# New due times for the steps behind the first weight loads in a fused attention and feed-forward kernel

## The chip, the cores and the metric

One Trainium2 chip, one of its cores. The metric is device microseconds (us) of one execution, the median of a few runs; lower is better. The profile is of one execution on that core.

## What is computed

A gated linear attention (RWKV style) over 4 batches, 8 heads, 768 positions and 48 values a head, whose output goes straight into a two-layer feed-forward net with 3072 tokens, width 384 and 2048 hidden values:

```python
for t in range(S):
    cur = np.einsum('bhd,bhe->bhde', u[None] * kt, vt)
    y[:, :, t] = np.einsum('bhd,bhde->bhe', rt, state + cur)
    state = wt[:, :, :, None] * state + np.einsum('bhd,bhe->bhde', kt, vt)
x = y.transpose(0, 2, 1, 3).reshape(B * S, H * D)
h = x @ w_in
g = np.maximum(0.01 * h, h)
return g @ w_out
```

Inputs and output are float32 in DRAM; the products run in bf16 and are summed in float32.

## The kernel before, in words

The 768 positions of each batch are cut into 6 chunks of 128, so there are 24 chunks, numbered in the order in which they are worked on. Chunks 0 to 3 are done two at a time (`pair`), chunks 4 to 23 one at a time (`single`). The work on a chunk of `single` is a chain over five engines:

1. SP issues four loads of 192 KB (w, k, r, v; L755) into one of 10 `in` tiles.
2. ACT takes the logarithm of w (`lw`, L765); PE sums it along the chunk (L771, L774, the step `cum`); DVE forms `ci` (L783); ACT takes the exponentials (L792, L797, L801); DVE multiplies them with r and k (L459).
3. The products are turned around, either on PE (L470, `tpose`) and copied out by DVE or ACT (L475, L477), or by a transposing DMA that SP issues (L818; the set `RK_DMA` says for which chunks).
4. PE forms the scores (L912), DVE masks them (L842, two instructions a chunk), PE forms the chunk's output (L878, L883, the step `intra`). Beside it PE forms the sum for the state (L852, `sums`), DVE adds it to the state (L867) and POOL scales the state for the next chunk of the batch (L829).
5. POOL works out the bonus term of u: `ru` (L489, L493), then DVE a reduction `dg` (L497), then POOL `vs` (L501); POOL also casts v (L509). DVE adds `vs` to the output (L532) and the sum y is turned into a column of `xT`, by PE (L518, the step `typose`, and a copy L523 or L525) or by a transposing DMA (L897; the set `Y_DMA`).

The feed-forward net works on blocks of one or two chunks: `up` (L1074) needs the block's columns of `xT`, ACT applies the leaky relu (L1089), `down` (L1104) sums over 16 products in four steps, DVE or ACT copies the result into one of 5 `o` tiles (L1115, L1117), and SP stores it (L1121). The last three blocks of two chunks each save one of eight products (`seven`: L1006 on PE, sums L989 on DVE, the final additions L1027 and copies L1020 and L1022, stores L1057). For them DVE forms differences of the weights beforehand (L958, four instructions).

No loop sets the order of all this. Every piece is a step (1089 of them) with the engines that may do it, an assumed duration, a due time and its dependencies. `Plan.order` plays the steps through once at build time: whenever an engine is free it takes the ready step with the lowest due time, and this gives the order in which the instructions are written into each engine's queue. Each engine then works its own queue strictly in that order, and an instruction that waits holds up all behind it. The table `RANK` is added to the due times by step number, and `FORCE` fixes the engine of some steps; a step without an entry keeps the due time that the code gave it:

```python
for i, x in RANK.items():
    plan.steps[i][2] = round(plan.steps[i][2] + x, 3)
for i, e in FORCE.items():
    plan.steps[i][0] = {e: plan.steps[i][0][e]}
order = plan.order(pools)
```

Two more things matter below. A transfer of SP goes into one queue of the DMA engines; in the middle of the kernel it lands about 4 us after its issue. And the PSUM tiles `ps` are 8 banks of 512 floats: in `seven`, one bank holds two results side by side (`px` and `py` in the first, `pv` and `pw` in the second).

Of the kernel before, what the change touches and what calls it, by code (L numbers as in the profile page):

```python
# [23 lines left out]
class Plan:  # L24
# [202 lines left out]
FORCE = {23: "DVE", 26: "DVE", 29: "ACT", 30: "DVE", 46: "ACT", 58: "ACT", 61: "ACT", 79: "ACT", 85: "DVE",  # L227
    112: "DVE", 114: "ACT", 117: "DVE", 119: "ACT", 121: "ACT", 123: "DVE", 125: "POOL", 127: "ACT", 128:
    "POOL", 134: "POOL", 137: "DVE", 139: "POOL", 142: "ACT", 143: "POOL", 492: "DVE", 500: "ACT", 604: "DVE",
    612: "ACT", 904: "DVE", 910: "DVE", 932: "ACT", 952: "ACT", 966: "ACT", 1002: "ACT", 1030: "ACT", 1075:  # L230
    "ACT", 1080: "ACT"}


@with_exitstack
# [946 lines left out]
```

## Time and profile before

| | us |
|---|---|
| median of 3 runs (180.39 to 180.79) | 180.65 |
| the profiled execution | 181.35 |
| its span, first to last instruction | 179.64 |
| PE busy in the span | 172.6 |
| DVE busy | 132.2 |
| ACT busy | 115.7 |
| POOL busy | 104.0 |

The profiled execution is 0.70 us above the median, and 1.71 us of it lie outside the span. "Busy" of PE counts the modelled end of each matmul, which overlaps the start of the next; what PE loses is therefore read from the starts of the matmuls: where one group begins later than the group before it takes elsewhere, PE has waited. SP's transfers are issued one behind the other from the start up to about 154 us; the share of the DMA engines in part 2 of the page is the packets' time, not their peak rate.

### The profile page before, as it was taken

What the parts mean: (1) busy time and instruction counts of PE and PEld (TensorE: products, weight loads), DVE (VectorE), ACT (ScalarE), POOL (GpSimd) and SP (SyncE); (2) the same over time, 40 slices, a digit from 0 to 9 for tenths busy, and PEclk for the clock granted to TensorE, in tenths of its full rate; (3) what the DMA queues carried; (4) which work ended last, traced back from release to release, by engine and by line L of the source; (5) the groups of instructions that cost most, each with busy time, mean ns of one, the idle gap of its engine ahead of it and who ended that gap; (6) DMA issues with size and microseconds to landing.
All of it is one profiled execution on the core that took longest, in us unless ns stands there. A gap on an engine that the chain in (4) does not pass through costs nothing.

```text
span 179.6 us, 5374 instructions
## 1 busy us (share of the span) xinstructions
PE 172.6 (96%) x2109; PEld 135.2 (75%) x2109; DVE 132.2 (74%) x265; ACT 115.7 (64%) x257; POOL 104.0 (58%) x138
## 2 busy tenths in 40 slices
PE   7998999999999999999999999999999999999991
PEld 2475878867878687787688777677778798899991
DVE  7589974189788898559687659499787599777472
ACT  2568968865957786895379775177675487735620
POOL 5989631675896486878468855414995459200000
PEclk9999999999999999999999999999999999999999
DMA  5999999999999989999899999999599996613004
GB/s 139 261 283 314 370 380 362 176 203 208 215 195 202 192 192 150 183 199 182 193 214 177 218 164 214 212 192 144 117 201 145 198 234 170 153 24 115 0 22 153
DMA packets 116715, 34.43 MB, mean 192 GB/s; under 512 B 109137, under 2 KB 115922, under 8 KB 116690
## 3 DMA queue, kind: packets, MB, share of 16 engines
q1 hardware_dynamic: 116688, 34.09, 90.8%
q8 instruction: 16, 0.26, 0.6%
q14 instruction: 9, 0.07, 0.1%
q10 hardware_dynamic: 2, 0.00, 0.0%
HBM read 25.17 MB, written 4.72 MB: 166 GB/s over the span
## 4 chain that ended last, share of the span: by engine, by line
PE 64%; DVE 8%; DMA 8%; ACT 6%; issue 5%; SPq 4%; POOL 3%; DVEq 0%; ACTq 0%; POOLq 0%
PE ps L1074 26%; PE ps L1104 17%; PE ps L1006 6%; DMA in<-in_w_dram 6%; SPq L755 3%; PE ps L1146 3%; PE ps L912 2%; DMA xT<-y 2%; DVE m L842 2%; POOL ru L489 1%; DVE o L1027 1%; ACT g L1089 1%; PE ps L883 1%; ACT rkT L477 1%; DVE m L690 1%
## 5 line engine op out<-in xcount | busy, mean ns | idle before, releaser
L1074 PE MATMUL ps<-xT,w_in_b 128*128 128x256 bf16 (+1 forms) x720 | 73.1, 251 | 0.4 <-ACT xT L525 0.2
L1089 ACT ACTIVATE g<-ps 128x512 bf16<-128x512 f32 x96 | 56.4, 595 | 20.6 <-PE ps L1074 15.3
L1074 PEld LDWEIGHTS <-w_in_b 128*128 128x128 bf16 x720 | 57.7, 98 | 9.3 <-issue 0.7
L1104 PE MATMUL ps<-w_out_b,g 128*128 128x384 bf16 x288 | 56.0, 326 | 0.1
L1104 PEld LDWEIGHTS <-g 128*128 128x128 bf16 x288 | 25.7, 97 | 12.4 <-ACT g L1089 0.2
L489 POOL TENSOR_TENSOR ru<-in,ub 128x384 f32<-128x384 f32 x24 | 24.5, 1027 | 10.9 <-DMA in<-in_k_dram 10.1
L459 DVE TENSOR_TENSOR rk<-in,ps 128x384 bf16<-128x384 f32 x46 | 24.3, 548 | 7.8 <-ACT ps L797 4.2
L842 DVE TENSOR_TENSOR m<-ps,maskb 128x512 bf16<-128x512 f32 x40 | 25.4, 683 | 6.1 <-PE ps L912 5.0
L493 POOL TENSOR_TENSOR ru<-ru,in 128x384 f32<-128x384 f32 x24 | 24.6, 1030 | 2.9 <-DMA in<-in_r_dram 2.2
L829 POOL TENSOR_TENSOR sb<-s,a 128x384 bf16<-128x384 f32 x18 | 15.7, 873 | 9.5 <-ACT a L792 9.4
L501 POOL TENSOR_TENSOR vs<-in,dg 128x384 f32<-128x384 f32 x20 | 16.6, 828 | 7.1 <-DVE dg L497 4.7
L509 POOL CAST vb<-in 128x384 bf16<-128x384 f32 x24 | 12.0, 503 | 11.3 <-DMA in<-in_v_dram 7.5
L783 DVE TENSOR_TENSOR ci<-ps,lw 128x384 f32<-128x384 f32 x20 | 11.1, 554 | 4.3 <-PE ps L771 1.9
L497 DVE TENSOR_REDUCE dg<-ru 128x8 f32<-128x384 f32 x24 | 12.9, 545 | 1.0 <-POOL ru L493 0.8
L765 ACT ACTIVATE lw<-in 128x384 bf16<-128x384 f32 x20 | 10.4, 520 | 3.6 <-DMA in<-in_w_dram 3.6
L797 ACT ACTIVATE ps<-ps 128x384 f32<-128x384 f32 x20 | 9.5, 475 | 4.2 <-DVE ci L783 3.8
L532 DVE TENSOR_TENSOR y<-ps,vs 128x384 bf16<-128x384 f32 x20 | 11.1, 553 | 1.5 <-PE ps L883 0.6
L867 DVE TENSOR_TENSOR s<-ps,sb 128x384 f32<-128x384 f32 x14 | 7.7, 552 | 4.0 <-PE ps L852 2.8
L801 ACT ACTIVATE ps<-ci 128x384 f32<-128x384 f32 x20 | 9.8, 488 | 0.6 <-DVE ci L783 0.6
L1146 PE MATMUL ps<-zeros 128*128 128x128 bf16 (+1 forms) x40 | 8.7, 339 | 1.3 <-DVE zeros L332 1.3
L525 ACT COPY xT<-ps 128x384 bf16<-128x384 bf16 x11 | 5.2, 481 | 6.8 <-PE ps L518 6.7
L792 ACT ACTIVATE a<-ps 64x4 f32<-64x4 f32 x36 | 6.0, 168 | 5.3 <-DVE ci L783 3.5
(105 smaller groups left out, 228.7 us busy)
## 6 DMA issues: line engine op xcount, KB each, us to landing
out_dram<-o SPq DMA_DIRECT2D x23, 192.0 KB, 3.2
in<-in_w_dram SPq DMA_DIRECT2D x20, 192.0 KB, 4.3
in<-in_k_dram SPq DMA_DIRECT2D x20, 192.0 KB, 4.2
in<-in_r_dram SPq DMA_DIRECT2D x20, 192.0 KB, 4.1
in<-in_v_dram SPq DMA_DIRECT2D x20, 192.0 KB, 4.3
in<-in_moe_w_out_dram SPq DMA_DIRECT2D x4, 768.0 KB, 12.3
in<-in_moe_w_in_dram SPq DMA_DIRECT2D x4, 384.0 KB, 7.0
in<-in_moe_w_in_dram SPq DMA_DIRECT2D x2, 768.0 KB, 9.8
```

The lines of the kernel that those rows point to most:

```text
L459: (nc.gpsimd if e == "POOL" else nc.vector).tensor_tensor(out=o, in0=x, in1=i, op=ALU.mult)
L489: lambda e: nc.gpsimd.tensor_tensor(out=ru.t[:], in0=kv(), in1=ubv, op=ALU.mult),
L493: lambda e: nc.gpsimd.tensor_tensor(out=ru.t[:], in0=ru.t[:], in1=rv(), op=ALU.mult),
L497: lambda e: nc.vector.tensor_reduce(out=dg.t[:], in_=ru.t[:], axis=AX.X, op=ALU.add),
L501: lambda e: nc.gpsimd.tensor_tensor(out=vs.t[:], in0=vv(), in1=dg.t[:].unsqueeze(2).to_broadcast([128, H, D]), op=ALU.mult),
L509: {"POOL": 0.56}, lambda e: nc.gpsimd.tensor_copy(out=vb.t[:], in_=vv()),
L829: lambda e: nc.gpsimd.tensor_tensor(out=sb.t[:].rearrange("p g a d -> p (g a) d"), in0=s_in.t[:].rearrange("p g a d -> p (g a) d"), in1=a_ ...
L842: lambda e, par=par: nc.vector.tensor_tensor(out=m.t[:, par, :, :], in0=sc[par].t[:].rearrange("p (g t) -> p g t", g=NP), in1=maskb[:].uns ...
L1074: nc.tensor.matmul(hp.t[:, a * N : (a + 1) * N], lhsT=w_in_b[:, t, (j + a) * 128 : (j + a + 1) * 128], rhs=xT[:, t, c0 : c0 + N], start=(a ...
L1089: lambda e, hp=hp, g=g, j=j, J=J, N=N: nc.scalar.activation(out=g.t[:, j : j + J, 0:N], in_=hp.t[:, 0 : J * N].rearrange("p (a n) -> p a n ...
L1104: nc.tensor.matmul(op.t[:, 0:DM], lhsT=g.t[:, j, off : off + 128], rhs=w_out_b[:, j, :], start=(j == 0), stop=(j == NJ - 1))
L1146: nc.tensor.matmul(warm.t[:, 0:n], lhsT=zeros[:, 0:128], rhs=zeros[:, 0:n], start=True, stop=True, skip_group_check=True)
```

## The change

The table `RANK` grows from 512 to 1008 entries, and 864 entries are new or have another value; all of them belong to steps from number 165 on. Up to there (chunks 0 to 3, the loads of all weights, and the first half of chunk 4) nothing is different. Before, the middle part (steps 144 to 490, which are chunks 4 to 14, and 716 to 900, which are feed-forward blocks 0 to 7) had no entries at all. `FORCE` fixes the engine of 24 more steps, frees three and turns two over. No step is added or removed. Of the diff, a small part:

```diff
-    143: -47.83, 491: 891.86, 492: -139.67, 493: -7.6, 494: -7.59, 497: 881.86, 498: -149.67, 499: 881.58,
...
+    143: -47.83, 165: -80.37, 166: -174.74, 169: 1102.4, 170: -174.74, 171: 1136.06, 172: -196.91, 178:
...
+    137.32, 325: 3.91, 326: 5.24, 327: 2.12, 328: 22.16, 329: 45.63, 330: -124.8, 331: 1047.38, 332: 128.33,
...
+    -187.78, 424: 96.31, 425: -227.49, 426: -245.49, 427: 1067.58, 428: 135.12, 429: -153.16, 430: 1079.26,
...
+    46.89, 768: 78.57, 769: 62.2, 770: -140.75, 771: 302.68, 772: 57.67, 773: -133.52, 774: 53.68, 775:
...
+    149.29, 1065: 206.32, 1066: 246.3, 1067: 169.3, 1068: 225.45, 1069: 220.75, 1070: 99.37, 1071: 97.38,
+    1072: 4.66, 1073: 175.78, 1074: 217.79, 1075: -15.34, 1076: -146.38, 1077: 218.76, 1078: -148.78, 1079:
...
-    "POOL", 134: "POOL", 137: "DVE", 139: "POOL", 142: "ACT", 143: "POOL", 492: "DVE", 500: "ACT", 604: "DVE",
-    612: "ACT", 904: "DVE", 910: "DVE", 932: "ACT", 952: "ACT", 966: "ACT", 1002: "ACT", 1030: "ACT", 1075:
-    "ACT", 1080: "ACT"}
+    "POOL", 134: "POOL", 137: "DVE", 139: "POOL", 142: "ACT", 143: "POOL", 186: "DVE", 188: "ACT", 197: "DVE",
+    201: "DVE", 237: "DVE", 253: "DVE", 277: "DVE", 279: "ACT", 310: "ACT", 324: "DVE", 342: "ACT", 383:
+    "ACT", 419: "DVE", 435: "DVE", 492: "ACT", 500: "DVE", 612: "ACT", 756: "DVE", 784: "ACT", 820: "ACT",
+    848: "ACT", 876: "DVE", 910: "DVE", 938: "ACT", 952: "ACT", 966: "ACT", 997: "DVE", 1002: "ACT", 1030:
+    "ACT", 1033: "ACT", 1038: "ACT", 1072: "ACT", 1075: "ACT", 1080: "ACT"}
```

Step numbers that are spoken of below: 326 and 327 are the k and r loads of chunk 10; 424 is the reduction `dg` of chunk 13; 757, 771, 785 and 799 are the stores of chunks 2, 3, 4 and 5; in the last block 1073 is the addition on DVE that reads the second half of the first bank, 1074 the products on PE that go into its first half, 1081 an addition on DVE that reads the first half of the second bank, and 1082 the last products on PE, which go into its second half.

How the change moves instructions can be listed from the two built programs, engine by engine. PE's queue is the same up to 41.6 us of the profile; from there 215 of its 320 steps stand in another place. On DVE 182 of 247 steps move, on ACT 181 of 258, on POOL 79 of 120, on SP 97 of 144 (from its 30th transfer on). Thirteen copies and sums go from ACT to DVE and eight from DVE to ACT. Every matmul of before is there once, and so is every transfer.

151 rows, old and new, of the table RANK are left out of this document.

## Prediction

> **What bounds the kernel now.** I read the busy shares first, then PE's starts, then the chain of work that ended last.
>
> ```profile
> span 179.6 us, 5374 instructions
> PE 172.6 (96%) x2109; PEld 135.2 (75%) x2109; DVE 132.2 (74%) x265; ACT 115.7 (64%) x257; POOL 104.0 (58%) x138
> PEclk9999999999999999999999999999999999999999
> ```
>
> PE is busy 96% of the span at a granted clock of 1.00 throughout, and no other engine passes 74%. So PE's own matmuls set the time, and a new order can gain only what PE waits. The 40 matmuls of zeros and everything up to 41.6 us stay as they are. Behind that I compared each group's start with the next one's: six matmuls of 256 columns take 0.655 us, four of 384 take 0.65. Two places where more passes:
>
> ```profile
> 61.42 0.82 PE L1104 MATMUL ps<-w_out_b,g 128*128 128x384 bf16 x4
> 62.45 0.92 PE L1074 MATMUL ps<-xT,w_in_b 128*128 128x256 bf16 x7 [0.20 <-ACT xT L525]
> ```
> ```profile
> 70.36 0.33 PE L518 MATMUL ps<-ident,y 128*128 128x128 bf16 x3
> 70.98 0.32 PE L771 MATMUL ps<-lw,trev 128*128 128x384 bf16 x1 [0.29 <-ACT lw L765]
> ```
>
> From 61.42 to 62.45 are 1.03 us instead of 0.65: PE waited 0.38 for a column of xT. From 70.36 to 70.98 are 0.62 instead of 0.17: 0.45 for a logarithm. All such excesses up to 172 us: 0.28 at 53.1, 0.38, 0.07 at 75.3, 0.45, 0.08 at 88.8, 0.16 and 0.22 at 131.7 and 132.6, 0.09 at 140.6, 0.27 at 149.5: **2.0 us**; at 175 us come 0.48 more. Beside these, about 0.1 us passes at each of the 12 groups of scores (L912) left; these groups remain, so this does too. The chain of work shows what is late at the first and third place:
>
> ```profile
> 47.92 4.93 DMA in<-in_w_dram
> ...
> 53.51 0.32 PE ps L771
> ...
> 65.24 5.14 DMA in<-in_w_dram
> 70.41 0.53 ACT lw L765
> ```
>
> The load of w lands, ACT turns it into the logarithm in 0.53 us, and PE is already there. Most of the chain is PE's own work, and DMA appears where a load was just in time.
>
> **The change, queue by queue.** Everything is set against the profiled execution: 181.35 us, 179.64 of them span. It lies 0.70 above the median of 180.65; I carry differences in the span over to the median. *Work*: the same 2109 matmuls and the same transfers, so nothing. DVE gets five instructions more and ACT five fewer, copies of 0.36 to 0.6 us on engines with 26% and 36% to spare: below 3 us of DVE, hidden under PE's work; without that cover they count once each in the masks' way (below).
>
> *SP's queue.* In the stretch from 43 to 121 us landings follow each other in the mean 1.06 us apart for a load (56), 0.87 for a store, 1.19 for a transposed rk, 0.55 for a transposed y. I walked the new list with these. Stores go back (chunk 2's from place 35 to 51, chunk 3's from 39 to 107, chunk 4's from 45 to 73, chunk 5's from 53 to 75), loads come forward: w of chunk 9 from place 44 to 39, 11 from 54 to 50, 13 from 63 to 53, 15 from 76 to 64, 17 from 87 to 79. Only chunk 10 is put back (w 49 to 54, k 50 to 56), since PE now takes chunk 11 first. Between the landing of w and PE's `cum` lay 0.6 to 0.8 us for chunks 7, 8, 11 and 12; in the new lists 0.4 (chunk 7, hardly moved), 3.1, 1.7, 2.0, and elsewhere 1.0 (chunk 10) to 14. Logarithm and semaphores need 0.6. So the waits on w go. The moved loads find their `in` tile free: each tile's former chunk is done 10 us or more earlier. The stores keep `o` tiles longer; tightest are chunk 9's copy, which reaches the head of DVE's queue at 90.4 while the store before it lands at 89.6, and chunk 8's on ACT (92.1 against 91.5). Transposing DMAs hold SP until their data is there: xT of chunk 10 until about 83.7 where SP would be at 82; four transfers are in flight then (4 us from issue to landing), so the stream thins but doesn't end. Cost 0; at the other end, if the tiles or waits bite, the 2 us of the worst gap between landings.
>
> *PE, DVE, ACT and POOL.* With normal group lengths I added up PE's new queue and laid each chunk's chain beside it. Where it is tight: DVE must add vs to y (0.55 us, and some 0.35 from matmul start to DVE and back) between a chunk's last products (L883) and their turning (L518). That gap falls from 1.3 to 1.7 us to 0.8 (chunks 7, 15, 19) and 1.0 (6, 13), but grows for chunk 18 (0.9 to 1.7). At a gap of 0.9 the present trace waits 0.09, so I put 0.2 on each 0.8 and 0.1 on each 1.0: 0.8 us. Masks of chunks 8 and 9 stand behind copies and dg on DVE: 0.3. Together **1.1 us of new waits**, on bounds of 0 (all meet) and about 2.9 (the widest gap between two landings, 2.85, falls on one of them); I take 1.1 as it is nearest to rows with the same pattern.
>
> *The tail.* One bank of PSUM is in question:
>
> ```profile
> 172.64 1.01 DVE L1027 TENSOR_TENSOR o<-ps,o 128x192 f32<-128x192 f32 x3 [0.84 <-PE ps L1006]
> ...
> 174.65 0.32 ACT L1022 COPY o<-ps 128x192 f32<-128x192 f32 x1 [1.30 <-DVE o L1027]
> 175.53 0.82 PE L1006 MATMUL ps<-w_out_b,in 128*128 128x192 bf16 x8 [0.32 <-DVE o L1027]
> ```
>
> DVE's first addition (step 1073) waits 0.84 for products (1074) that go into the other half of its bank. The new order writes 1073 ahead of 1074, so PE waits for DVE: the copy starts 0.25 behind the products of 1070, takes 0.32, the addition 0.36, with semaphores 1.03; PE has one group of 0.66 in between: 0.37 lost. The last products (1082) still wait for 1081: copy and f2 (1076) and addition end 1.41 behind 1079, PE has 1.00 of work: 0.41 instead of 0.48. Tail: **0.78 instead of 0.48**. The Trainium skill ("PSUM — Partial Sum Buffer", section "PSUM bank collisions raise a hardware error") says that two engines may not touch one bank in the same partitions at once, so accesses must be ordered by bank, not by address; that speaks against this swap. The trace's 0.84 agrees; with ordering by address the 0.37 would be nil and the sum 0.37 lower.
>
> *Sum*: -2.0 + 0.30 + 1.1 = **-0.6 us**: 180.75 for the profiled execution, 180.0 for the median.
>
> **The rivals.** *All meets.* The new waits are nil, as on paper the gaps allow, and -1.7 remain: 178.95. For it speaks that PE, when late once, gives all the rest more room; against it the five gaps of 0.8 to 1.0.
>
> *Waits only change places.* New waits of 1.7 us: 180.65, the change shifts the loads as it says and PE doesn't notice, since copies and masks take the place of loads. For it: only 0.73 of the 2.0 us were waits on w.
>
> *DVE behind POOL at 72 to 84 us: slower.* In DVE's new queue the reductions dg of chunks 10 and 13 stand ahead of the four masks (L842) for the scores of chunks 10 and 11. They need POOL.
>
> ```profile
> L489 POOL TENSOR_TENSOR ru<-in,ub 128x384 f32<-128x384 f32 x24 | 24.5, 1027 | 10.9 <-DMA in<-in_k_dram 10.1
> L842 DVE TENSOR_TENSOR m<-ps,maskb 128x512 bf16<-128x512 f32 x40 | 25.4, 683 | 6.1 <-PE ps L912 5.0
> L493 POOL TENSOR_TENSOR ru<-ru,in 128x384 f32<-128x384 f32 x24 | 24.6, 1030 | 2.9 <-DMA in<-in_r_dram 2.2
> ```
>
> POOL already waits 10.1 us for loads of k at L489. Chunk 10's k, now the 56th transfer, lands at 44.0 + 24 loads, a store and two transposes = 72.0. Behind it POOL has four of 1.03 (L489 and L493, chunks 10 and 13) and one of 0.87: 77.0. Then DVE: dg 0.55, a copy 0.55, four masks of 0.68, two more of 0.55: 82.0. PE needs the masks at 82.05, and with the waits and score gaps before it at about 83.2. So k may be 1.2 us late; beyond that PE loses every further 1 us. Eleven of 76 landings came more than 1.5 us behind the one before, up to 2.85; two such delays (1.8 each over the mean) cost 2.4: 182.4, one and a late neighbour 1.2 to 1.8: about 181.8 as the middle. Against it: r of both chunks and k of 13 are there early.
>
> **Chances.** The forecast 0.46 (its own range 179.4 to 180.4), all meets 0.13, waits only change places 0.15, DVE behind POOL 0.20, a slower case that I haven't seen 0.06. This measurement can tell about 0.2% (0.36 us) from no change. Of the forecast's 0.46 some 0.42 lie below 180.3 and 0.04 within: faster 0.55, same 0.19, slower 0.26. The range 178.9 to 182.0 leaves out the best end of "all meets" (0.05) and the worse half of the slow cases (0.13).
>
> **What will show it.** Right: PE's starts have no excess at `cum` of chunks 8 and 11; L755's landings of w lie over 1 us ahead of L771; PE waits at L518 of chunks 7, 15 and 19 by up to 0.2; in the tail PE waits for L1027 before step 1074 and again before the last group (1082), which starts at about 174.9 instead of 175.53. Wrong: a wait over 0.5 us between 76 and 84 us at L883 behind DVE's L842, with POOL's L489 waiting for k before it; a copy L1115 or L1117 that waits for a store; or SP idle for several us before L818 or L897, with loads landing later than by the list. If PE's starts behind 41.6 us show excesses of 2 us or more again, the second rival is right. I am wrong altogether if the sum of excesses falls and the time doesn't follow.

## The result, and the profile after

The changed kernel takes 181.05 us (median of 20 runs, 180.63 to 182.14); the kernel before took 180.70 us beside it (20 runs, 180.3 to 181.2). The ratio is 1.0026, 95% interval [1.0015, 1.0037]: **slower by about a quarter of a per cent**. The forecast was 180.0 us, and faster.

The profiled execution tells it the other way round. That of the changed kernel took 180.68 us, 0.67 less than the profiled execution of before and almost the 0.6 less of the forecast; but it lies at the lower end of its 20 runs, and that of before (181.35) above all 20 of its kernel. Nor is the 0.67 the gain that was forecast: of the 0.66 in the span, 0.51 is an earlier start of the part that the change touches and 0.30 a shorter end, while PE's waits rose by 0.15 us, from 2.72 to 2.87 (table below). First lines of the page of the kernel after: the span, the busy shares and the granted clock.

```profile
span 179.0 us, 5375 instructions
PE 171.9 (96%) x2108; PEld 134.6 (75%) x2109; DVE 134.0 (75%) x270; ACT 113.3 (63%) x252; POOL 103.7 (58%) x138
PEclk9999999999999999999999999999999999999999
```

PE still bounds the kernel, at full clock. The places where PE waited in before, in PE's timeline of after (start, us, engine, line):

```profile
64.84 0.36 PE L947 MATMUL ps<-vb,m 128*128 128x48 bf16 x8
65.04 0.81 PE L1138 MATMUL ps<-xT,w_in_b 128*128 128x256 bf16 x6
```
```profile
67.61 0.82 PE L1138 MATMUL ps<-xT,w_in_b 128*128 128x256 bf16 x6
68.26 0.33 PE L835 MATMUL ps<-lw,trev 128*128 128x384 bf16 x1
```

L1138, the first group of block 5, follows its forerunner without a gap (0.38 in before), and `cum` of chunk 11 starts 0.65 behind the group ahead of it, its plain length (0.46 waited in before). The loads came early, as forecast: from the landing of w to `cum` now pass 3.3 us for chunk 8, 2.0 for chunk 11, 2.3 for chunk 12. The other old waits went too, and new ones came. They stand in PE's waits view (engine, line, who is waited for; total, times, longest):

```profile
PE ps L1070 <- DVE o L1091: 0.4, 2, 0.3
PE ps L1168 <- ACT g L1153: 0.4, 1, 0.4
PE ps L916 <- POOL vb L573: 0.3, 1, 0.3
```

This view counts only what lies between records; from start to start PE lost 0.36 and 0.42 us at the first, 0.60 at the second, and 0.51 and, behind it, 0.27 more at the third. The chain of work that ended last passes through both middle places, first at 97 us, then at 125 to 132 us:

```profile
96.69 0.51 ACT g L1153
97.21 0.37 ACT xT L589
97.58 0.51 ACT g L1153
...
98.13 0.50 PE ps L1168 x2
```
```profile
125.03 1.70 POOL ru L557
126.73 1.18 POOL vb L573
127.90 0.79 POOL vs L565
128.69 0.95 POOL ru L553
...
129.72 1.01 POOL ru L557
...
130.76 0.03 DVE dg L561
...
131.23 0.56 DVE rk L523
...
131.82 0.83 PE ps L1138 x12
```

At 97 us a copy of xT stands between two g on ACT, and PE waits for the second. At 125 to 132 us five POOL instructions in a row, then DVE, set when PE goes on. The first two of the five are longer than their kind. The timeline of all engines shows what DVE does in their time:

```profile
124.50 1.37 DVE L1022 TENSOR_TENSOR in<-w_out_b,in 128x1536 bf16<-128x1536 bf16 x1
...
125.02 1.71 POOL L557 TENSOR_TENSOR ru<-ru,in 128x384 f32<-128x384 f32 x1
...
126.26 1.28 DVE L1022 TENSOR_TENSOR in<-w_out_b,in 128x1536 bf16<-128x1536 bf16 x1
...
126.67 1.23 POOL L573 CAST vb<-in 128x384 bf16<-128x384 f32 x1
```

L1022 forms two of the differences of the weights. Beside them `ru` takes 1.71 us and the cast 1.23, where the median of their lines is 1.00 and 0.50: 1.44 us more on POOL, in all nine profiles of the changed order and its variants. In the kernel before two instructions of POOL are as long beside such differences, at 121.3 us (1.63 for 0.83) and 126.2 us (1.71 for 1.00), but PE didn't wait for it there. That the two engines hold each other up is read from this overlap; no run moves them apart.

The tail, in the timeline of all engines (weight loads left out):

```profile
170.44 0.82 PE L1070 MATMUL ps<-in,in 128*128 128x192 bf16 x8
...
171.04 0.36 DVE L1091 TENSOR_TENSOR o<-ps,o 128x192 f32<-128x192 f32 x1 [0.32 <-ACT o L1086]
...
171.46 1.48 PE L1070 MATMUL ps<-in,in 128*128 128x192 bf16 x16 [0.19 <-DVE o L1091]
```

PE's group of 0.66 starts at 170.44, the next (1074) at 171.46: 0.36 lost behind DVE's addition 1073, against 0.37 forecast. The last group (1082) loses 0.42 (0.41 forecast).

The row of the masks, before which DVE had sat idle for 6.1 us:

```profile
L906 DVE TENSOR_TENSOR m<-ps,maskb 128x512 bf16<-128x512 f32 x40 | 25.6, 684 | 3.5 <-PE ps L976 3.4
```

Before it DVE now waits for PE alone, 3.5 us. The feared case of DVE behind POOL at 72 to 84 us did not come in this profile: k of chunk 10 landed at 72.3 (72.0 forecast), and PE has no excess from 76 to 84 us.

### The profile page after: what moved, and what is told of

It is laid out like the page before. It is cut to its first block, busy times and chain, and to the rows that moved or that the text cites. A ratio compares the mean times of both kernels' runs of the same rounds, so it can differ in the third digit from the quotient of the medians.

```text
span 179.0 us, 5375 instructions
## 1 busy us (share of the span) xinstructions
PE 171.9 (96%) x2108; PEld 134.6 (75%) x2109; DVE 134.0 (75%) x270; ACT 113.3 (63%) x252; POOL 103.7 (58%) x138
## 4 chain that ended last, share of the span: by engine, by line
PE 72%; DVE 7%; POOL 5%; DMA 5%; ACT 4%; SPq 3%; issue 3%; DVEq 0%; ACTq 0%; POOLq 0%
PE ps L1138 29%; PE ps L1168 21%; PE ps L1070 7%; DMA in<-in_k_dram 3%; PE ps L976 3%; SPq L608 3%; PE ps L534 2%; POOL ru L557 2%; DVE m L906 2%; PE ps L947 2%; DVE rk L523 2%; PE ps L835 1%; PE ps L942 1%; PE ps L916 1%; DVE ci L847 1%
## 5 line engine op out<-in xcount | busy, mean ns | idle before, releaser
L1138 PE MATMUL ps<-xT,w_in_b 128*128 128x256 bf16 (+1 forms) x720 | 73.0, 251 | 0.2
L1138 PEld LDWEIGHTS <-w_in_b 128*128 128x128 bf16 x720 | 57.3, 98 | 8.0 <-issue 0.5
L553 POOL TENSOR_TENSOR ru<-in,ub 128x384 f32<-128x384 f32 x24 | 23.9, 1000 | 15.5 <-DMA in<-in_k_dram 9.0
L557 POOL TENSOR_TENSOR ru<-ru,in 128x384 f32<-128x384 f32 x24 | 25.2, 1058 | 3.4 <-DMA in<-in_r_dram 2.7
L573 POOL CAST vb<-in 128x384 bf16<-128x384 f32 x24 | 12.8, 534 | 6.6 <-DMA in<-in_v_dram 6.6
L1181 ACT COPY o<-ps 128x384 f32<-128x384 f32 x10 | 4.8, 478 | 7.7 <-PE ps L1168 7.6
L1210 PE MATMUL ps<-zeros 128*128 128x128 bf16 (+1 forms) x39 | 8.0, 322 | 1.3 <-DVE zeros L396 1.3
```

The source lines that it names most:

```text
L553: lambda e: nc.gpsimd.tensor_tensor(out=ru.t[:], in0=kv(), in1=ubv, op=ALU.mult),
L557: lambda e: nc.gpsimd.tensor_tensor(out=ru.t[:], in0=ru.t[:], in1=rv(), op=ALU.mult),
L573: {"POOL": 0.56}, lambda e: nc.gpsimd.tensor_copy(out=vb.t[:], in_=vv()),
L1138: nc.tensor.matmul(hp.t[:, a * N : (a + 1) * N], lhsT=w_in_b[:, t, (j + a) * 128 : (j + a + 1) * 128], rhs=xT[:, t, c0 : c0 + N], start=(a ...
```

## The experiments

Below, "waits" are PE's excesses from start to start, small ones counted, less 0.1 us for each change to scores.

**One profile, or the kernel?** The two kernels were run again, unchanged, in three sets. First set:

> The kernel before, unchanged, against itself: a control of the timing, and a second profile. Theory A (the profiled execution of before at 181.35 us was one of its slow ones, so part of the 2.0 us of waits that I counted was chance): the ratio lies at 1.000 within 0.0005, and the new profile shows fewer waits of PE behind 41.5 us, in sum about 0.65 us less than the 2.7 (small ones counted) of the first. Theory B (the waits are fixed by the order; the profile was only late from its start): the same places with the same waits within 0.1 us each, and the span differs by when the step behind the first weight loads starts.

> The changed kernel, unchanged: a second profile, and its ratio in this set of runs. Theory A (new named waits of fixed size): 1.0026 again, with PE waiting 0.6 us at L1168 for the g behind xcopy of chunk 13, 0.5 and 0.3 us at L916 for vb of chunk 19, and 0.36 and 0.42 us in the tail, each within 0.1. Theory B (chance: landings of loads that vary): ratio 1.0026, but the waits of 0.5 us and more lie elsewhere than in the first profile; only the tail's stay.

Measured: before against itself 1.0012 [0.9994, 1.0029] (its profiled execution took 437 us and is left out); the changed kernel 1.0045 [1.0022, 1.0067]. Its second profile has 0.60 at 97 us, 0.50 and 0.26 at 131, 0.36 and 0.42 in the tail: all five within 0.02 of the first. They belong to the order. But up to 91 us it waits 1.03 instead of 0.43, among it 0.41 and 0.23 at 48 to 49 us (the logarithm of chunk 7, whose w landed at 48.1 instead of 47.4, and a g behind it on ACT).

> The kernel before once more, unchanged, since the first repeat left no usable profile. Theory A (waits fixed by the order): PE's waits at 53, 61, 70, 131, 132, 149 and 174 us stand where they stood, each within 0.1 us of 0.28 (up to 0.5 with a late load), 0.38, 0.46, 0.16, 0.22, 0.27 and 0.49, and the step behind the first weight loads starts 0.3 to 0.5 us earlier than the 41.58 us of the first profile, as in the four others. Theory B (the first profile had waits by chance): the sum is lower by 0.65 us. The ratio is 1.000 within its interval.

Measured: 0.9997 [0.9984, 1.0009]. The waits at 61, 131, 140, 149 and 174 us stand within 0.01; that before `cum` of chunk 8 is 0.35; that of chunk 11, 0.46 in the first profile, is **gone**, and 0.57 stand at another step of chunk 11. So each theory holds for half of the waits: those on copies and banks are fixed, those on loads change places from run to run.

> The kernel before, one more profile. PE's waits from 41.5 to 91 us were 1.39 and 1.97 us in its two profiles, 0.81 and 0.82 from 91 to 168 us, 0.52 in the tail. Theory A (the profiles were slow executions): 0.8 to 1.3 us up to 91 us, with a time near 180.7; 0.8 and 0.52 behind it. Theory B (1.4 to 2.0 is usual): 1.4 or more again, with a time of 181.2 or more.

> As for the third profile of the kernel before: theory A 0.8 to 1.3 us of waits up to 91 us, theory B 1.4 or more; 0.8 us and 0.52 behind it by both.

> The changed kernel, one more profile. PE's waits from 41.5 to 91 us were 0.43 and 1.03 us in its two profiles. Theory A: around 0.6 us, with 1.65 from 91 to 168 us and 0.78 in the tail as before, and a time near 181.05. Theory B: as low as 0.4 in most executions; then the time would lie at 180.7, below its measured median.

> As for the third profile of the changed kernel: theory A around 0.6 us of waits up to 91 us, theory B 0.4; 1.65 and 0.78 us behind it by both.

All four profiles of each unchanged kernel (us; "start" is that of chunk 4's scores, step 164, ahead of anything the change moved; "end" runs from the start of 1082 to the end of the span; the third and fourth of each ran on one chip):

| execution | time | start | waits to 91 | 91 to 168 | tail | end |
|---|---|---|---|---|---|---|
| before 1 (the page shown) | 181.35 | 39.78 | 1.39 | 0.81 | 0.52 | 4.11 |
| before 2 | 181.17 | 38.99 | 1.97 | 0.82 | 0.52 | 4.12 |
| before 3 | 180.47 | 39.19 | 1.02 | 0.82 | 0.52 | 4.12 |
| before 4 | 180.63 | 39.18 | 1.19 | 0.81 | 0.52 | 4.13 |
| after 1 (the page shown) | 180.68 | 39.27 | 0.43 | 1.66 | 0.78 | 3.81 |
| after 2 | 181.36 | 39.34 | 1.03 | 1.65 | 0.78 | 3.81 |
| after 3 | 180.58 | 39.27 | 0.25 | 1.65 | 0.78 | 3.82 |
| after 4 | 181.47 | 39.26 | 1.21 | 1.63 | 0.78 | 3.82 |

Span less start and waits is 137.14 to 137.19 in before's four and 136.84 to 136.89 in after's: nothing else varies. For the kernel before theory A is right; of the changed kernel's two new ones, 0.25 and 1.21, neither is A's 0.6 nor B's 0.4. The page that I predicted from was a late one twice over: its start by 0.6 us and its waits up to 91 us by 0.2 to 0.4, against the two executions near the median. In the third profile of before, `cum` of chunk 11 (L771) follows without a gap:

```profile
70.08 0.33 PE L518 MATMUL ps<-ident,y 128*128 128x128 bf16 x3
70.25 0.33 PE L771 MATMUL ps<-lw,trev 128*128 128x384 bf16 x1
```

The means of the four: waits to 91 us 1.39 and 0.73 (-0.66), from 91 to 168 us 0.82 and 1.65 (**+0.83**), tail +0.26, end -0.30: +0.13 in sum, as the means of their times (180.91 and 181.02). The 20 timed runs show 0.35 between the medians; four executions that spread over 0.9 us can't tell this from 0.13. An estimate from the table closes the account: with the 1.72 us outside the span, a start of 39.2 and the other columns as they are, the medians of 180.70 and 181.05 stand for waits of 1.3 and 0.8 us up to 91 us, so -0.5, +0.83, +0.26 and -0.30 give +0.3.

How a late load reaches PE is seen in the fourth profile of the changed kernel:

```profile
70.96 0.55 DVE L561 TENSOR_REDUCE dg<-ru 128x8 f32<-128x384 f32 x1 [0.99 <-POOL ru L557]
...
72.36 0.35 DVE L587 COPY xT<-ps 128x384 bf16<-128x384 bf16 x1
...
72.76 0.92 PE L1138 MATMUL ps<-xT,w_in_b 128*128 128x256 bf16 x7 [0.42 <-DVE xT L587]
```

r of chunk 11 landed at 69.8 us (68.0 in the first profile). POOL's second product waited for it, DVE's reduction dg of chunk 11 for POOL, and behind dg on DVE stood the copy of xT that PE needed: 0.56 us lost. That is the mechanism of the rival "DVE behind POOL", at a copy instead of the masks, in one of four executions.

**The tail alone, both ways.** One step is moved in the finished order; all queues stay as they are.

```diff
 # in the changed kernel (aft_tailold); in the kernel before (bef_tailnew) 1073 is put ahead of 1074
         order = plan.order(pools)
+        order.remove(1073)
+        order.insert(order.index(1074) + 1, 1073)
```

> The changed order with one step moved: 1073 (DVE's addition on one half of a PSUM bank) is written behind the products 1074 into its other half, as in the kernel before. DVE's and PE's own queues are the same; only who waits for whom is turned round. My theory of the tail: PE's 0.36 us before 1074 goes, the wait before 1082 becomes 0.48 instead of 0.42, so 0.30 us less than the changed kernel: ratio about 1.0009 against before. Rival (the end is set by the copies, additions and the store behind the last products, and DVE's addition that now waits takes back what PE gains): no gain, ratio 1.0026.

> The kernel before with that one step moved the other way: the addition 1073 ahead of the products 1074, all queues otherwise the same. My theory of the tail: 0.30 us more, ratio 1.0017, with PE waiting some 0.37 us before 1074. Rival: no difference, ratio 1.000 within 0.0005.

Measured: the changed kernel with the old tail 0.9998 [0.9982, 1.0014], the old kernel with the new tail 1.0023 [1.0004, 1.0043]. In the profiles PE's wait before 1074 is gone in the one and 0.40 us in the other. My theory of the tail holds in both directions, its rival falls: this one step is worth about what the whole change lost. By the clock it is worth more than the 0.30 us (0.0017) forecast, 0.0023 in the one and 0.0047 in the other against the changed kernel of the same set (1.0045), with intervals of about 0.002 to either side; the waits on loads in these runs are part of that. The wait before 1082 stayed at 0.41 with the old tail, where I expected 0.48. The line in the old kernel with the new tail:

```profile
172.35 0.82 PE L1006 MATMUL ps<-in,in 128*128 128x192 bf16 x8 [0.24 <-DVE o L1027]
```

The Trainium skill ("PSUM — Partial Sum Buffer", section "PSUM bank collisions raise a hardware error") has accesses ordered by bank and not by address. The built program is ordered so, as both runs show: 1073 and 1074 touch different halves, the list of steps has no dependency between them, and PE waits nonetheless. What would happen without that wait no run shows.

**The two new waits in the middle.** At 97 us: `up` of block 7, group j4 (860), and the products that need its g (873) stood 15 places apart in PE's queue in before, 4 in after; and the copy of chunk 13's xT (443), on DVE before, now runs on ACT ahead of that g (861). At 130 us: on POOL the cast vb of chunk 19 (581) now stands behind both products of chunk 20 (628, 629).

```diff
         order = plan.order(pools)
+        order.remove(861)
+        order.insert(order.index(443), 861)
+        order.remove(581)
+        order.insert(order.index(629), 581)
 # aft_all has two more:
+        order.remove(1073)
+        order.insert(order.index(1074) + 1, 1073)
+        order.remove(219)
+        order.insert(order.index(229) + 1, 219)
```

> The changed order with two steps moved on their own engines. On ACT, g of step 860 (861) stands ahead of the copy of chunk 13's xT (443) instead of behind it; on POOL, the cast vb of chunk 19 (581) stands ahead of the second product of chunk 20 (629) instead of behind it. Theory A (two short gaps in the new queues cost what PE waited there): the wait of 0.60 us at 97 us falls to about 0.2, those of 0.50 and 0.26 at 130 and 131 us to 0.1 or less together; in sum about 1.0 us less than the changed kernel, ratio about 0.997 against before. Theory B (what PE gains there it waits a little later, for a load or for the step that was pushed back): both waits go, others of the same size come within the next 15 us, ratio 1.0026 again.

> The same two moves, and two more: the addition 1073 behind the products 1074 as in the kernel before, and on DVE the reduction dg of chunk 6 (219) behind ci of chunk 7 (229). Theory A: beside the 1.0 us, 0.30 us of the tail and the 0.2 us before tpose of chunk 7 go; 1.5 us less than the changed kernel, ratio about 0.994 against before. Theory B: only the tail's 0.3 us goes, ratio about 1.000.

Measured: 1.0024 [1.0006, 1.0041] and 1.0002 [0.9988, 1.0016]. A miss, and theory B by the time. At 97 us the wait fell to 0.21 as expected. At 130 the 0.50 went, but the 0.27 behind it grew to 1.09. The chain of the first of the two kernels shows why:

```profile
129.96 1.00 POOL ru L557
...
130.98 0.04 DVE dg L561
...
131.45 0.56 DVE rk L523
...
132.05 0.83 PE ps L1138 x12
```

The `up` group L1138 needs a PSUM tile that DVE's product rk of chunk 21 (646) frees; ahead of that on DVE stands the reduction dg of chunk 20 (630); and dg needs POOL's product 629, which I had pushed back behind a cast of 0.50 us. So 0.77 us of waits became 1.09, which is about what was gained at 97 us. In the second kernel the 0.22 before `tpose` of chunk 7 went and 0.35 appeared at its `sums`, which wait for v. So one link more was cut:

```diff
+        order.remove(630)
+        order.insert(order.index(646) + 1, 630)
 # and 861, 581 and 1073 as above (219 stays)
```

> The changed order with the tail put back (1073 behind 1074), g 861 ahead of the copy 443 on ACT, vb of chunk 19 ahead of the product 629 on POOL, and now also the reduction dg of chunk 20 (630) behind the product 646 of chunk 21 on DVE. In the earlier run without that last move the 0.50 us at 130 us went and the 0.27 at 131 us grew to 1.09: PE's up group waits for a PSUM tile that 646 frees, 646 stands behind 630 on DVE, and 630 waits for POOL's 629, which had been pushed back. Theory A (one chain over three queues; with its last link cut the time comes): nothing over 0.25 us is waited between 128 and 134 us, 0.4 us at 97 and 0.3 us of the tail go too, 1.0 to 1.4 us less than the changed kernel, ratio 0.995 to 0.997. Theory B (waits only change places): the wait stands at yet another step behind 131 us, and the ratio is that of the tail alone, 1.000.

Measured: 179.71 us, **0.9943 [0.9927, 0.9958]**. Theory A holds. PE's timeline has no gap at 130 to 132 us now, its waits from 91 to 168 us are 0.81 instead of 1.65 (0.30 appear at 135 us), and the kernel is faster than both. POOL's two long instructions stand there as before (1.72 and 1.23 us), so they alone don't make PE wait; whether keeping DVE's additions away from them would have done as well wasn't tried. PE's timeline:

```profile
130.33 0.50 PE L916 MATMUL ps<-vb,rk 128*128 128x96 bf16 x8
130.67 0.83 PE L1138 MATMUL ps<-xT,w_in_b 128*128 128x128 bf16 x12
131.34 0.33 PE L835 MATMUL ps<-lw,trev 128*128 128x384 bf16 x1
```

**The last group in its own bank.**

```diff
+            last = nb == len(blocks) - 1
+            b4 = Buf("ps", "op3") if last else b2
 # pw, the products s_3 (start=last) and the addition s_c12 use b4 instead of b2
```

> The same four moves, and the last group of products (1082) in a PSUM bank of its own instead of the other half of the bank that the addition 1081 reads; the order of all queues is unchanged. Theory A (PE waits before the last group because of the shared bank, not because of its data): the 0.42 to 0.49 us before 1082 go, the end comes 0.4 us earlier than without, ratio 0.993 to 0.995. Theory B (the end is set by DVE's additions and the stores): PE's wait goes, the span doesn't follow, same ratio as without.

> The kernel before with w of chunks 8 and 11 loaded earlier (as in the earlier run, ratio 0.9998 there) and the last group in a PSUM bank of its own. Theory A: 0.49 us of the tail go: ratio 0.997, and PE's starts show nothing before 1082. Theory B: 1.000.

The second of the two also has the two loads of w ahead that stand under "Loads alone". Measured: 0.9944 [0.9924, 0.9965] (179.51 us) and 0.9989 [0.9973, 1.0005]. PE's wait before 1082 is gone in both (0.03 left in the tail), so the bank was its cause. The time hardly follows: in the first, what passes behind the last addition grew from 2.60 to 2.82 us, half of the gain: its last stores are issued closer together, and the last packet lands 1.54 us behind the addition instead of 1.30. In the second it stays as it was. The rest is below what 6 and 12 runs tell. Inconclusive for the time.

**Loads alone.** In the kernel before, two loads of w go ahead; in another, four stores are left out.

```diff
 # bef_w_early
+        order.remove(262)
+        order.insert(order.index(224), 262)
+        order.remove(348)
+        order.insert(order.index(326), 348)
 # bef_no_stores
+        order = [i for i in order if i not in (757, 771, 785, 799)]
```

> The kernel before with two loads of w moved ahead on SP's queue and nothing else: w of chunk 8 ahead of r and v of chunk 7 (two loads earlier), w of chunk 11 ahead of k, r and v of chunk 10 (four transfers earlier). This is what the change does to the loads that PE waited for, alone. Theory A (a wait on w goes when the load goes ahead, and the loads pushed back have room): the waits before cum of chunk 8 (0.28 to 0.51 us) and of chunk 11 (0.46 to 0.51) go, 0.75 to 1.0 us less, ratio about 0.995. Theory B (the loads are short of room as a stream: the ones pushed back are waited for instead): waits of the same sum stand at other steps of chunks 7, 10 or 11, ratio 1.000.

> The kernel before without the stores of chunks 2 to 5 (places 34, 38, 44 and 52 of SP's queue): four blocks of 128 rows of the output are left out, all else is the same. The question is what makes PE wait for loads between 47 and 76 us, at other steps in every profile (0.9 to 1.4 us in sum). Theory A (the stream of transfers is full there, so an order only chooses which load is late): the loads behind come up to 3.5 us earlier, the waits on loads between 47 and 76 us go, 0.7 to 1.2 us less, ratio about 0.995; the waits at 61 (xT), 131, 149 and 174 us stay. Theory B (SP's queue, held at the transposes until their data is there, sets the landings): the landings behind each transpose hardly move, the waits stay, ratio 1.000.

Measured: 0.9998 [0.9983, 1.0012] and 0.9983 [0.9970, 0.9996]. With the loads ahead the wait of 0.28 to 0.51 before `cum` of chunk 8 is gone, and 0.37 stand before `sums` of chunk 7, whose v was pushed back: theory B, as far as the time tells (0.26 stood at that place in the fourth profile of the unchanged kernel, too). Without four stores the waits up to 91 us are 0.59, and 0.3 us of time go (interval 0.1 to 0.5), less than A's 0.7 and more than B's nothing; but one profile can't be set against four here, since the last group's kernel with all its stores (bef_best) has 0.6 as well. The landings show that each theory has a part. Two stores less stand ahead of the transposing DMA at 48.7 us, but it holds SP for 2.82 us now (1.64 to 2.37 in the profiles of before), and the load behind it is issued at 51.6 instead of 51.7 to 52.4: most of what the stores freed is lost there. Loads right behind it hardly come earlier, as in theory B, but not for B's reason: DVE had written its data by 48.7 us. Farther on w of chunk 11 lands at 67.0 (68.0 to 70.4) and w of chunk 12 at 72.1 (74.7 to 75.4), as in theory A. So the transfers ahead do limit this stretch; the size is about 0.3 us, not 1.

## Why the prediction was wrong, point by point

*The bound* was right: PE, and only its waits matter.

*-2.0 us of old waits.* All nine went, as forecast. But the sum came from one execution. (At 88.8 us the list has 0.08 where the starts give 0.18; with small ones counted the sum is 2.20.) The fixed part (0.38 at 61 us, 0.82 behind 91 us) is real; of the waits on loads, the 0.46 at `cum` of chunk 11 stood in one of four profiles of the kernel before (and, at 0.51, in that with the new tail), and other loads are late in its place. After the change 0.25 to 1.21 us of waits still stand up to 91 us in four executions. Net, the stretch to 91 us gained 0.66 in the mean of four, not the 1.26 of my list.

*1.1 us of new waits: the step that failed.* I put 0.8 on five gaps between a chunk's products and their turning, and 0.3 on masks. Of that 0.07 came, at the turning of chunk 19. What came is 1.65 us behind 91 us, 1.37 of it at two places that I had counted as hidden or hadn't looked at: a copy of xT that changed engines and now stands ahead of g on ACT while PE's distance between g's group and its user shrank from 15 places to 4; and a cast behind two products on POOL. The sentence "copies of 0.36 to 0.6 us on engines with 26% and 36% to spare ... hidden under PE's work" is where the first was lost: a share of idle time says nothing about the one instruction behind which another stands. I had walked SP's queue and the y chain; I had not walked ACT's g and POOL's vb. And "with normal group lengths" a walk of POOL would have put vb of chunk 19 at up to 1.44 us earlier (an estimate from the two long instructions), about 1 us before PE needs it: the place shows only with the lengths that POOL has beside DVE's additions. The runs show the cost: with those repaired, 0.84 us of waits and 1.0 us of time (against the kernel with the old tail, which is level with before) go.

*The tail, +0.30.* Right: 0.26 in the profiles, 0.36 and 0.42 at the two places (0.37 and 0.41 forecast), and in time by undoing it and by doing it alone, though there larger than the forecast. With the measured middle, +0.17 (-0.66 and +0.83) instead of -0.9, the same sum would have forecast a loss of 0.47.

*Carrying the span's difference over to the median* failed by itself. The profiled execution of before lay 0.65 above the median, and I saw that; it came from its start and from loads that were late by chance. (180.65 less 0.6 is 180.05; the forecast gives it as 180.0.) Subtracting fixed gains from 180.65 while counting chance waits of a late execution among them counts the lateness twice.

*Rivals.* "Waits only change places" (180.65, chance 0.15) was the nearest in mechanism: middle sums of 2.20 and 2.09 in the two pages. It took the middle as a gain of 0.3 (-2.0 and 1.7), which with the tail came out at nothing; the four profiles of each show +0.17 there. "All meets" didn't come. "DVE behind POOL" came in one execution of four, 0.56 us and at a copy, not at the masks. The slower time itself falls to the case that I hadn't seen (0.06).

*Not foreseen:* from the end of the last addition to the end of the span pass 2.58 to 2.61 us in the changed order and 2.88 to 2.91 in the old, two modified kernels apart (2.82 and 2.98). It took 0.3 us off the loss. The stores don't land sooner: the last packet lands 1.29 to 1.31 us behind the addition in both. The difference lies in the closing barrier, whose instructions the views leave out: in the trace's own records 0.33 to 0.35 us pass between POOL's last drain and its next semaphore instruction in all eight profiles of the old order and 0.04 in all nine of the changed one, though all that it waits for has come. POOL has 198 records in the one and 208 in the other; whether that is the reason wasn't tried. The forecast said nothing of it, so this part is luck.

## What to carry to other kernels

Before an excess is called a gain to be had, see it in two or three executions: waits between engines repeat to 0.02 us, waits on loads wander. When an order is rewritten, walk every in-order queue past each moved step, the lightly loaded ones too, and follow a late step over all its links (here POOL, DVE, a PSUM tile, PE): cutting one link made 1.09 us of 0.77 at the next, cutting both gave the time back. And lay the row of an instruction at its place beside its median: two of POOL's took 1.44 us more beside DVE's large additions. Two engines on the halves of one PSUM bank are one dependency more, and which is written first decides who pays for it.

## What the runs showed of the hardware that was not expected

The same kernel, unchanged and at full clock, has between 0.25 and 1.21 us (after) and between 1.02 and 1.97 (before) of waits in the stretch from 41.5 to 91 us, where loads are just in time, while the rest behind its start repeats within 0.05 us; that alone spreads the time by some 0.9 us. POOL's `ru` and cast took 1.71 and 1.23 us instead of 1.00 and 0.50 while DVE added two bf16 tiles of 128x1536, in nine of nine profiles, and DVE's two took 1.37 and 1.28 us where others of the line took 0.95. The first transposing DMA held SP's queue for 1.6 to 3.2 us at 48 to 50 us, the loads behind it with it, though its data had been written when it began; those behind 150 us took 1.2 to 1.3. The end of the program took 0.3 us more in the old order, in POOL's part of the closing barrier. And taking 0.42 us of PE's wait out of the last group gave 0.2 us back at the end in one of two kernels.
